# Splits of the experts' weights, each placed behind a named ACT instruction and spread over more steps

## The chip, the cores and the metric

One Trainium2 chip, and one of its cores. The metric is the device time of one execution of the kernel in microseconds (us). The engines are TensorE (PE; PEld are its weight loads), VectorE (DVE), ScalarE (ACT), GpSimd (POOL) and SyncE (SP), whose queue issues most of the DMA transfers.

## What is computed

The reference runs three layers one after the other, all in float32. Cut to what matters:

```
k_s, q_s = softmax(k over the sequence), softmax(q over the head)     # 8 batches, 8 heads, 576 x 64
x   = q_s @ (k_s^T @ v)                                               # 4608 tokens x 512
logits = x @ w_gate + log1p(exp(x @ w_noise)) * noise                 # 8 experts, the best 2 of each token
out[token] += weight * (relu(x @ w1[e]) @ w2[e])                      # w1 512 x 1024, w2 1024 x 512
h   = out @ w_in;  result = (h * cos(h)) @ w_out                      # w_in 512 x 2048, w_out 2048 x 512
```

## The kernel before

**Stages.** The span falls into these stretches. From 0 to some 125 us the keys and values are loaded and the products k^T v are formed, together with the first 18 of 36 "query columns" of 128 tokens. From 125 to some 255 us the other 18 columns follow: for each, x_t transposes 128 tokens on PE (L368), ACT takes the exponential of the transpose (tile qtt, L370), x_mm multiplies (L384, L389), and DVE divides and reduces (L392 to L398). Routing, the choice of two experts for each token, runs in three chunks beside them: the first covers columns 0 to 17, and its chain goes from ACT (L432 to L437: rs, ru, rt, rln) to DVE (L441 to L463) to ACT (rex, L469) to DVE and PE, to ACT again (W, L488) and to DVE, and it ends with a list of rows, idx (L543). With that list POOL gathers tokens for the first expert (tile xg, L618). Every token group passes an expert in "steps" of 128 of the hidden columns: mm1 (PE, L750 to L752) fills ph, ACT makes the rounded half hh of it (L756), DVE the rest hl (L757), and two steps later (LAG = 2) mm2 (L774 to L776) multiplies hh and hl by w2 into acc. At a group's end the accumulators are copied to ys, those with an even number by ACT (L785) and those with an odd number by DVE (L787). The groups of the first expert hold 2, 2, 2 and 3 blocks of 128 tokens, those of the seven others 4, 3 and 2; a tenth block is computed only when an expert has that many tokens. Each has 8 steps. The last layer runs in the same manner, as 9 groups of 4 blocks and 16 steps, with more work on ACT and DVE (kk, r) between ph and hh; its weights count as "experts" 8 and 9.

**Weights and splits.** Every weight is used as a rounded half (float32r) and a rest, w = h + l. An expert's weights come in 16 pieces of 128 x 512: SP loads a piece into one of three staging tiles wst (L141), ACT copies it to w1h or w2h, which rounds (L136), and POOL subtracts, w1l or w2l (L137). That pair is called a split here. The generator w_load has a piece loaded at each of its steps and splits the piece loaded two steps before. wbg.step(n) advances it by n: by 4 for each query column (expert 0), by 2 for each step of the first expert's last group and of the last layer, by 1 for each step of the others.

**What else runs beside the experts.** DVE turns w_in and w_out, which come as float64, into float32: 64 jobs of eight instructions (L821 to L833), whose inputs SP loads (tile c, L844) and whose results SP writes (L834, to wi_d and wo_d). They run beside the first experts only. SP also carries the DMA transposes of the gathered tokens (L645).

**Order.** Each engine works through its own queue in order. A scheduler sets that order when the program is built: it takes the instructions as the Python code issues them, simulates them, and places each where its simulation finds the engine free. `tc.issue_after(i)` bars it from placing an instruction ahead of instruction i. The transposes L677 were already placed in this way.

Of the kernel before, what the change touches and what calls it, by code (L numbers as in the profile page):

```python
# [15 lines left out]
AF = mybir.ActivationFunctionType  # L16
# [11 lines left out]
def tile_attention_moe_moe2(  # L28
# [14 lines left out]
    nc = tc.nc  # L43
# [70 lines left out]
        return res  # L114

    W = [None, None]

    def alloc_w(pool, i):
        w1h = pool.tile([P, NK, F], F32R, name=f"w1h{i}")
# [5 lines left out]
    def w_load(e):  # L125

        pend = []
        w1h, w1l, w2h, w2l = W[e % 2]

        def split():  # L130
            (kind, i, fh, _), st = pend.pop(0)
            if kind == 0:
                hi, lo = w1h[:, i, fh * 512:(fh + 1) * 512], w1l[:, i, fh * 512:(fh + 1) * 512]
            else:
                hi, lo = w2h[:, i, :], w2l[:, i, :]
            nc.scalar.activation(hi, st, AF.Copy)  # L136
            nc.gpsimd.tensor_tensor(lo, st, hi.bitcast(F32), op=ALU.subtract)  # L137

        for pc in w_pieces(e):
            st = late[0].tile([P, 512], F32, name="wst", bufs=3)  # L140
            nc.sync.dma_start(st, pc[3])  # L141
            pend.append((pc, st))
            if len(pend) == 3:
                yield
                split()
        while pend:
            yield
            split()
# [209 lines left out]
    def x_t(n):  # L358

        t, c9 = divmod(n, PC)  # L360
        pt = ps_at("pqt", "tr", 2)
        for i in range(4):
            if c9 < 8:
                b, c = 2 * t + c9 // 4, c9 % 4
                src = QE[2 * b + i // 2][:, c, 2 * (i % 2):2 * (i % 2) + 2, :]
            else:
                src = QTL[t][:, 2 * i:2 * i + 2, :]
            nc.tensor.transpose(pt[:, i * P:(i + 1) * P], src.rearrange("p h d -> p (h d)"), ident)  # L368
        qtt = at.tile([P, 4, P], F32, name="qtt", bufs=2)
        nc.scalar.activation(qtt, pt.rearrange("p (i s) -> p i s", i=4), AF.Exp)  # L370
        QTT[n] = qtt

    def x_mm(n):
# [371 lines left out]
    def mm1(g, f):  # L745
        w1h, w1l = W[(g.e if g.t is None else f // NF) % 2][:2]
        fs = slice((f % NF) * P, (f % NF + 1) * P)
        ph = ps_tr("ph", g.i < NEARLY)[:, :g.N]
        for kc in range(NK):
            nc.tensor.matmul(ph, w1h[:, kc, fs], g.xh[:, kc, :g.N], start=kc == 0, stop=False)  # L750
            nc.tensor.matmul(ph, w1h[:, kc, fs], g.xl[:, kc, :g.N], start=False, stop=False)  # L751
            nc.tensor.matmul(ph, w1l[:, kc, fs], g.xh[:, kc, :g.N], start=False, stop=kc == NK - 1)  # L752
        j = steps.index((g, f)) % (LAG + 1)
        hh, hl = HH[j][:, :g.N], HL[j][:, :g.N]
        if g.t is None:
            nc.scalar.activation(hh, ph, AF.Relu)  # L756
            after.append(nc.vector.scalar_tensor_tensor(hl, ph, 0.0, hh.bitcast(F32), op0=ALU.max, op1=ALU.subtract))  # L757
        else:
            kk = late[1].tile([P, 512], F32, name="kk", bufs=2)
            r = late[1].tile([P, 512], F32, name="r", bufs=2)  # L760
            times_cos(r, kk, ph)
            nc.scalar.activation(hh, r, AF.Copy)  # L762
            after.append(nc.vector.tensor_tensor(hl, r, hh.bitcast(F32), op=ALU.subtract))  # L763
        HT[g.i, f] = (hh, hl)

# [119 lines left out]
    def experts():  # L885

        nonlocal over
        fbg = None
        first = NEARLY * NF
        for i in range(first, len(steps) + LAG):  # L890
            if i < len(steps):
                g, f = steps[i]
                if f == 0 and g.i > NEARLY and groups[g.i - 1].more:
                    last_block(groups[g.i - 1])
                mm1(g, f)
                if f == 0 and g.e == E - 1 and g.more:

                    nc.scalar.activation(spare, HT[g.i, f][0][:, :1].bitcast(F32), AF.Sin, scale=0.0)
            if i >= first + LAG:
                mm2(*steps[i - LAG])  # L900
            if i >= len(steps):
                continue
            nxt = groups[g.i + 1] if g.i + 1 < len(groups) else None
            if g.i == NEARLY:
                if f == 2:

                    nc.gpsimd.memset(YS[0], 0.0)
                    nc.sync.dma_start(y_d[(NB - 1) * P * E:, :].rearrange("(p j) d -> p j d", p=P),
                                      YS[0][:, None, :].to_broadcast([P, E, DM]))
                if f == g.nf - 2:  # L910
                    why = "a count of experts"
                    over = nc.values_load(flag[:1, :1], min_val=0, max_val=2 * E,
                                          skip_runtime_bounds_check_because=why)
                    for e in range(E):
                        used.append(nc.values_load(flag[:1, 1 + e:2 + e], engines=USERS, min_val=0, max_val=1,
                                                   skip_runtime_bounds_check_because=why))
                if f == g.nf - 1:
                    cbg.add(convert())
            if f == (2 if g.t == 0 else 0) and nxt is not None:
                fbg = fetch(nxt)  # L920
            if fbg is not None:
                if g.t is None or f % 2 == 0:
                    next(fbg, None)
            p0 = g.nf - (2 if g.nb > 2 else 1) - (nxt.nx if nxt else 0)
            if nxt is not None and f >= p0:
                if f == p0:
                    finish(fbg)
                    pbg = prep(nxt)
                next(pbg, None)
                if f == g.nf - 1:  # L930
                    finish(pbg)
            wbg.step(2 if g.t is not None or g.e == 0 else 1)
            if g.nb > 2 or f < p0:
                cbg.step(2 if f == 0 else 1)
            if f == g.nf - 1 and nxt is not None:
                if nxt.t == 0:
                    cbg.drain()
                    wbg.drain()
                    late.pop().release()
                    late.append(tc.alloc_tile_pool(name="tp", bufs=1, reuse_waits="tile"))  # L940
                    wbg.add(w_load(E + 1))
                elif nxt.t is None and nxt.b0 == 0 and nxt.e + 1 <= E:
                    wbg.drain()
                    if nxt.e + 1 == E:
                        cbg.drain()
                    wbg.add(w_load(nxt.e + 1))
# [64 lines left out]
    for n in range(n, NCOL):  # L1011
# [10 lines left out]
                if t + 1 < NPAIR:  # L1022
                    load_tail(t + 1, "q")
        x_unit(n)
        wbg.step(4)
        if n >= 27:
            bg.step(2)
            dbg.step(1 + n % 2)
# [27 lines left out]
    left = 0  # L1056
    while dbg.q:
        dbg.step()
        left += 1
        if left >= 3:  # L1060
            next(pg, None)
# [93 lines left out]
```

## Time and profile before

| | |
|---|---|
| time, median of 3 runs | 1932.73 us (1931.42 to 1937.19) |
| the profiled execution | 1936.69 us, of which the span of the trace 1934.6 us |
| PE busy | 1815.6 us, 94% of the span |
| DVE, ACT, POOL busy | 58%, 44%, 23% of the span |
| mean granted TensorE clock | 0.962 of full speed |

Busy shares are averages over the stretches above, which have different limits. The trace names for each idle time of an engine the event that ended it: "PE acc L776 <- DVE hl L757" is PE idle ahead of the matmul of line 776 until the DVE instruction of line 757 was done. The profiled execution took 3.96 us longer than the median of the runs.

### The profile page before, as it was taken

How to read it: one execution, taken by the hardware profiler on the slowest of the kernel's cores; microseconds unless marked ns; L12 is line 12 of the kernel's file. 1: busy time of each engine (PE TensorE's matmuls, PEld its weight loads, DVE VectorE, ACT ScalarE, POOL GpSimd, SP SyncE). 2: the span in 40 equal slices, each digit the busy share in tenths (PEclk: the TensorE clock that was granted, in tenths of full speed). 3: DMA queues.
4: the chain of work that ended last, by engine and by line, in shares of the span. 5: the costliest groups of instructions: out<-in, count | busy, mean ns of one | idle time of the engine just before them, and what ended most of it. 6: DMA issues, size and time to landing. Idle time of an engine off the chain costs nothing. (4 is left out here: it accounts for less than half of the span.)

```text
span 1934.6 us, 27003 instructions
## 1 busy us (share of the span) xinstructions
PE 1815.6 (94%) x9738; PEld 1531.3 (79%) x9738; DVE 1118.6 (58%) x2138; ACT 860.6 (44%) x1514; POOL 447.7 (23%) x405
## 2 busy tenths in 40 slices
PE   5875988999899999999999999999999999999998
PEld 4764877788787788888888878888888888888886
DVE  4657677877767744334323357665656566665654
ACT  5542223313123132232424256666666666666654
POOL 6655033404114023041405143110101010110000
PEclk8775999999999999999999999999999999999999
DMA  9954246546545443252435342211212030201000
GB/s 269 291 168 129 79 128 206 186 142 192 150 125 182 141 132 115 79 155 81 133 92 148 98 139 65 71 28 60 56 33 66 23 88 16 72 28 49 1 23 23
DMA packets 179774, 206.18 MB, mean 107 GB/s; under 512 B 34224, under 2 KB 121264, under 8 KB 179632
## 3 DMA queue, kind: packets, MB, share of 16 engines
q1 hardware_dynamic: 160704, 152.17, 26.4%
q0 software_dynamic: 12160, 39.86, 7.1%
q10 hardware_dynamic: 6768, 12.32, 1.7%
q8 instruction: 82, 1.34, 0.3%
q14 instruction: 60, 0.49, 0.1%
HBM read 127.06 MB, written 49.43 MB: 91 GB/s over the span
## 5 line engine op out<-in xcount | busy, mean ns | idle before, releaser
L750 PE MATMUL ph<-xh,w1h 128*128 128x512 f32 (+2 forms) x1376 | 491.9, 357 | 6.9 <-DVE r L696 2.9
L752 PE MATMUL ph<-xh,w1l 128*128 128x512 f32 (+2 forms) x1376 | 491.3, 357 | 0.0
L751 PE MATMUL ph<-xl,w1h 128*128 128x512 f32 (+2 forms) x1376 | 490.6, 357 | 0.0
L774 PE MATMUL acc<-w2h,hh 128*128 128x512 f32 x1152 | 455.8, 396 | 17.1 <-DVE ys L787 9.7
L775 PE MATMUL acc<-w2l,hh 128*128 128x512 f32 x1152 | 453.3, 394 | 0.0
L776 PE MATMUL acc<-w2h,hl 128*128 128x512 f32 x1152 | 427.7, 396 | 21.5 <-DVE hl L757 19.7
L750 PEld LDWEIGHTS ph<-xh,w1h 128*128 128x128 f32 x1376 | 261.8, 190 | 47.1 <-DVE hl L757 4.0
L751 PEld LDWEIGHTS ph<-xl,w1h 128*128 128x128 f32 x1376 | 261.5, 190 | 38.2 <-DMA xl<-xg 0.8
L752 PEld LDWEIGHTS ph<-xh,w1l 128*128 128x128 f32 x1376 | 261.8, 190 | 32.1
L776 PEld LDWEIGHTS acc<-w2h,hl 128*128 128x128 f32 x1152 | 217.2, 190 | 73.7 <-DVE hl L757 26.1
L774 PEld LDWEIGHTS acc<-w2h,hh 128*128 128x128 f32 x1152 | 218.2, 189 | 65.7 <-ACT hh L756 11.1
L775 PEld LDWEIGHTS acc<-w2l,hh 128*128 128x128 f32 x1152 | 218.4, 190 | 40.4
L757 DVE SCALAR_TENSOR_TENSOR hl<-ph,hh 128x256 fp32r<-128x256 f32 (+2 forms) x200 | 107.1, 538 | 243.3 <-ACT hh L756 243.1
L756 ACT ACTIVATE hh<-ph 128x256 fp32r<-128x256 f32 (+2 forms) x200 | 93.9, 472 | 265.2 <-PE ph L752 250.8
L696 DVE SCALAR_TENSOR_TENSOR r<-r,ph 128x512 f32<-128x512 f32 x144 | 98.9, 687 | 151.4 <-ACT r L695 150.3
L618 POOL DMA_INDIRECT xg<-x_d,idx x80 | 76.8, 959 | 441.8 <-DVE xl L681 190.4
L694 ACT ACTIVATE r<-r 128x512 f32<-128x512 f32 x144 | 90.7, 630 | 151.9 <-DVE r L693 151.9
L763 DVE TENSOR_TENSOR hl<-r,hh 128x512 fp32r<-128x512 f32 x144 | 102.1, 709 | 86.4 <-ACT hh L762 86.3
L680 ACT ACTIVATE xh<-xg 128x512 fp32r<-128x512 f32 x106 | 66.7, 630 | 166.2 <-DVE xg L677 164.0
L137 POOL TENSOR_TENSOR w1l<-wst,w1h 128x512 fp32r<-128x512 f32 x80 | 104.9, 1326 | 137.9 <-ACT w1h L136 137.0
L618 POOL DMA_INDIRECT xg<-y_d,SL x36 | 34.3, 954 | 420.5 <-DVE xl L681 389.8
L692 DVE SCALAR_TENSOR_TENSOR r<-kk,ph 128x512 f32<-128x512 f32 x144 | 98.7, 685 | 51.6 <-ACT kk L691 50.0
(186 smaller groups left out, 2162.9 us busy)
## 6 DMA issues: line engine op xcount, KB each, us to landing
wst<-in_moe_w_dram SPq DMA_DIRECT2D x128, 256.0 KB
xl<-xg SPq DMA_DIRECT2D x396, 64.0 KB
y_d<-ys ACTq DMA_DIRECT2D x47, 256.0 KB
kt<-in_k_dram SPq DMA_DIRECT2D x16, 512.0 KB
vt<-in_v_dram SPq DMA_DIRECT2D x16, 512.0 KB
qt<-in_q_dram SPq DMA_DIRECT2D x16, 512.0 KB
x_d<-xs SPq DMA_DIRECT2D x32, 256.0 KB
c<-in_moe_w_in_dram SPq DMA_DIRECT2D x32, 256.0 KB
```

Source lines behind the costliest of these rows:

```text
L137: nc.gpsimd.tensor_tensor(lo, st, hi.bitcast(F32), op=ALU.subtract)
L618: return nc.gpsimd.indirect_dma_start(out=dst, out_offset=None, in_=src, in_offset=bass.IndirectOffsetOnAxis(ap=ix, axis=0))
L692: nc.vector.scalar_tensor_tensor(r, kk, -C1, ph, op0=ALU.mult, op1=ALU.add)
L696: nc.vector.scalar_tensor_tensor(r, r, 1.0, ph, op0=ALU.subtract, op1=ALU.mult, reverse0=True)
L750: nc.tensor.matmul(ph, w1h[:, kc, fs], g.xh[:, kc, :g.N], start=kc == 0, stop=False)
L751: nc.tensor.matmul(ph, w1h[:, kc, fs], g.xl[:, kc, :g.N], start=False, stop=False)
L752: nc.tensor.matmul(ph, w1l[:, kc, fs], g.xh[:, kc, :g.N], start=False, stop=kc == NK - 1)
L757: after.append(nc.vector.scalar_tensor_tensor(hl, ph, 0.0, hh.bitcast(F32), op0=ALU.max, op1=ALU.subtract))
L763: after.append(nc.vector.tensor_tensor(hl, r, hh.bitcast(F32), op=ALU.subtract))
L774: nc.tensor.matmul(g.acc[m], hh[:, ms], w2h[:, fr, :], start=f == 0, stop=False)
L775: nc.tensor.matmul(g.acc[m], hh[:, ms], w2l[:, fr, :], start=False, stop=False)
L776: nc.tensor.matmul(g.acc[m], hl[:, ms], w2h[:, fr, :], start=False, stop=f == g.nf - 1)
```

## The change

A list named `behind` takes every exponential of a query column (L370) and every hh (L756, and L762 in the last layer). The ACT half of each split may not be placed ahead of the last entry of that list. Three rates change: a query column advances the weights of the first expert by 2 pieces in place of 4, a step of the first expert's last group advances those of the second by 1 in place of 2, and the loop that finishes the first expert's early groups now advances them too. No instruction is added or removed but for the waits that go with the order.

```diff
     W = [None, None]
+    behind = []
...
                 hi, lo = w2h[:, i, :], w2l[:, i, :]
-            nc.scalar.activation(hi, st, AF.Copy)
+
+            with tc.issue_after(behind[-1].ins):
+                nc.scalar.activation(hi, st, AF.Copy)
             nc.gpsimd.tensor_tensor(lo, st, hi.bitcast(F32), op=ALU.subtract)
...
         qtt = at.tile([P, 4, P], F32, name="qtt", bufs=2)
-        nc.scalar.activation(qtt, pt.rearrange("p (i s) -> p i s", i=4), AF.Exp)
+        behind.append(nc.scalar.activation(qtt, pt.rearrange("p (i s) -> p i s", i=4), AF.Exp))
...
-            nc.scalar.activation(hh, ph, AF.Relu)
+            behind.append(nc.scalar.activation(hh, ph, AF.Relu))
...
-            nc.scalar.activation(hh, r, AF.Copy)
+            behind.append(nc.scalar.activation(hh, r, AF.Copy))
...
-            wbg.step(2 if g.t is not None or g.e == 0 else 1)
+            wbg.step(2 if g.t is not None else 1)
...
         x_unit(n)
-        wbg.step(4)
+        wbg.step(2)
...
     while dbg.q:
         dbg.step()
+        wbg.step()
         left += 1
```

Line numbers of the changed kernel are 3 greater than those of the kernel before from the split on.

**ACT, query columns, start of the first routing chunk.** ACT's queue in the kernel before (L136 is the copy of a split, L370 a column's exponential, L432 to L437 the start of the routing):

```order
L136 ACTIVATE w1h_1668<-wst 128x512 x3
L370 ACTIVATE qtt<-pqt 128x512
L136 ACTIVATE w1h_1668<-wst 128x512
L370 ACTIVATE qtt<-pqt 128x512
L136 ACTIVATE w2h_1670<-wst 128x512 x2
L432 ACTIVATE rs<-lg 128x144
L433 ACTIVATE ru<-rs 128x144
L435 ACTIVATE rt_1750<-ru,one 128x144
L437 ACTIVATE rln<-rt_1750 128x144
```

The same place of ACT's queue in the changed kernel:

```order
L373 ACTIVATE qtt<-pqt 128x512 x2
L139 ACTIVATE w1h_1668<-wst 128x512
L435 ACTIVATE rs<-lg 128x144
L436 ACTIVATE ru<-rs 128x144
L438 ACTIVATE rt_1742<-ru,one 128x144
L440 ACTIVATE rln<-rt_1742 128x144
```

Six splits stood ahead of rln, one does now.

**ACT, the end of the same routing chunk's part on ACT**, from rex to W, in the kernel before:

```order
L469 ACTIVATE rex<-rdl 128x18
L136 ACTIVATE w1h_1668<-wst 128x512
L136 ACTIVATE w2h_1670<-wst 128x512 x3
L370 ACTIVATE qtt<-pqt 128x512
L136 ACTIVATE w2h_1670<-wst 128x512
L488 ACTIVATE W_71<-pr 128x18
```

And in the changed kernel:

```order
L472 ACTIVATE rex<-rdl 128x18
L139 ACTIVATE w2h_1670<-wst 128x512
L373 ACTIVATE qtt<-pqt 128x512
L139 ACTIVATE w2h_1670<-wst 128x512 x2
L491 ACTIVATE W_71<-pr 128x18
```

All 16 splits of the first expert stood ahead of W, seven do now. On POOL the rests move with them: four stood ahead of the first of the last subtractions for the query softmax (tile qe, L347), one does now, and the gathers of the first group (L618) stand behind 13 rests of 16, with three more behind the gathers, where all 16 stood long before them.

**ACT, the first steps of the second expert's first group** (4 blocks), in the kernel before (L785 is the copy of the group before, L790 its write, hh the rounded half of a step):

```order
L136 ACTIVATE w1h_1668<-wst 128x512 x3
L785 ACTIVATE ys_1683<-acc 128x512
L790 DMA y_d<-ys_1683 128x512
L136 ACTIVATE w1h_1668<-wst 128x512
L756 ACTIVATE hh_1677<-ph 128x512
L756 ACTIVATE hh_1675<-ph 128x512
L136 ACTIVATE w2h_1670<-wst 128x512
L785 ACTIVATE ys_1681<-acc 128x512
L136 ACTIVATE w2h_1670<-wst 128x512 x2
L790 DMA y_d<-ys_1681 128x512
L756 ACTIVATE hh_1676<-ph 128x512
```

And in the changed kernel:

```order
L139 ACTIVATE w2h_3114<-wst 128x512
L788 ACTIVATE ys_1683<-acc 128x512
L793 DMA y_d<-ys_1683 128x512
L139 ACTIVATE w2h_3114<-wst 128x512 x2
L759 ACTIVATE hh_1677<-ph 128x512
L759 ACTIVATE hh_1675<-ph 128x512
L139 ACTIVATE w1h_1668<-wst 128x512
L788 ACTIVATE ys_1681<-acc 128x512
L793 DMA y_d<-ys_1681 128x512
L759 ACTIVATE hh_1676<-ph 128x512
L139 ACTIVATE w1h_1668<-wst 128x512
L759 ACTIVATE hh_1677<-ph 128x512
```

The last four splits of the second expert's own weights (w2h_3114) now stand here, and from the second step on one split of the third expert's (w1h_1668) follows each hh; the 16 splits last for the 16 steps of the groups of 4 and 3 blocks, where they stood in the first 8 steps or so. The same holds for the experts after it. In the first steps of the last layer no split stands ahead of the first kk any more, where five did.

**DVE, the end of the second expert's group of 4 blocks**, in the kernel before (L757 is hl, L787 the copy of an accumulator, L821 and L822 begin a conversion job whose input SP loads):

```order
L757 SCALAR_TENSOR_TENSOR hl_1679<-ph,hh_1676 128x384
L757 SCALAR_TENSOR_TENSOR hl_1680<-ph,hh_1677 128x384
L821 TENSOR_SCALAR ca<-c_5321 128x256
L787 COPY ys_1683<-acc 128x512
L822 TENSOR_SCALAR ca<-ca 128x256
```

And in the changed kernel:

```order
L760 SCALAR_TENSOR_TENSOR hl_1679<-ph,hh_1676 128x384
L760 SCALAR_TENSOR_TENSOR hl_1680<-ph,hh_1677 128x384
L790 COPY ys_1683<-acc 128x512
L824 TENSOR_SCALAR ca<-c_5321 128x256
L825 TENSOR_SCALAR ca<-ca 128x256
```

The copy stood behind the first instruction of a conversion; it stands ahead of it now, and so at the same place of the third and the fourth expert. SP's loads of weights, which stood in bursts, are spread over the steps, and some stand among the DMA transposes of the groups. The order of PE's own instructions hardly changes.

## Rows read from the trace of the kernel before

**Rows 1.** The page's part 1: busy us, share of the span, instructions.

```profile
PE 1815.6 (94%) x9738; PEld 1531.3 (79%) x9738; DVE 1118.6 (58%) x2138; ACT 860.6 (44%) x1514; POOL 447.7 (23%) x405
```

**Rows 2.** Windows: stretch, us; PE, PEld, DVE, ACT, POOL busy; clock, DMA, GB/s.

```profile
125.00:199.00 74.00, 45.03 (x434) 37.95 (x431) 53.59 (x150) 21.88 (x45) 35.98 (x29) 0.63 0.45 137
199.00:255.00 56.00, 55.91 (x465) 47.87 (x464) 37.77 (x141) 13.97 (x34) 3.48 (x6) 1.00 0.19 63
255.00:335.00 80.00, 67.77 (x373) 58.76 (x372) 61.30 (x124) 23.81 (x46) 33.17 (x29) 0.96 0.59 192
335.00:700.00 365.00, 336.87 (x1655) 286.23 (x1655) 268.00 (x602) 95.53 (x191) 91.34 (x78) 0.97 0.52 159
700.00:1140.00 440.00, 439.70 (x2271) 383.45 (x2270) 151.50 (x238) 140.14 (x274) 125.21 (x108) 1.00 0.37 111
1140.00:1170.00 30.00, 24.81 (x99) 19.04 (x98) 22.65 (x23) 23.12 (x41) 23.33 (x20) 0.94 0.74 212
1170.00:1935.00 765.00, 756.07 (x3332) 624.93 (x3330) 449.91 (x668) 474.42 (x775) 59.22 (x57) 1.00 0.14 42
```

**Rows 3.** Waits, 125 to 199 us: waiter, releaser; us in total, times, longest.

```profile
PE pqt L368 <- ACT qtt L370: 18.2, 8, 4.9
...
ACT w1h L136 <- DMA wst<-in_moe_w_dram: 9.6, 4, 4.8
ACT w2h L136 <- DMA wst<-in_moe_w_dram: 8.6, 4, 3.7
```

**Rows 4.** Timeline of ACT, 139 to 165 us: start, us, instruction, [idle before, releaser].

```profile
139.97 0.63 ACT L136 ACTIVATE w1h<-wst 128x512 fp32r<-128x512 f32 x1 [4.80 <-DMA wst<-in_moe_w_dram]
...
162.50 1.31 ACT L136 ACTIVATE w2h<-wst 128x512 fp32r<-128x512 f32 x2 [3.73 <-DMA wst<-in_moe_w_dram]
...
164.71 0.18 ACT L488 ACTIVATE W<-pr 128x18 f32<-128x18 f32 x1
```

**Rows 5.** Timeline of DVE and POOL, 141 to 186 us.

```profile
143.84 1.22 DVE L344 TENSOR_REDUCE qm<-qt 128x16 f32<-128x1024 f32 x1 [5.36 <-POOL qe L347]
...
164.92 0.46 DVE L426 TENSOR_TENSOR rw<-rm,pr 128x288 f32<-128x288 f32 x1 [4.51 <-ACT W L488]
...
185.76 1.14 POOL L618 DMA_INDIRECT xg<-x_d,idx  x1 [12.63 <-DVE idx L543]
```

**Rows 6.** Waits of PE and ACT, 255 to 335 us.

```profile
ACT w2h L136 <- DMA wst<-in_moe_w_dram: 14.6, 5, 6.7
...
PE acc L776 <- DVE hl L757: 5.2, 2, 3.5
...
PE acc L774 <- ACT hh L756: 3.1, 3, 1.7
```

**Rows 7.** Waits of ACT and PE, 335 to 700 us.

```profile
ACT w2h L136 <- DMA wst<-in_moe_w_dram: 34.5, 17, 4.5
...
PE acc L776 <- DVE hl L757: 14.6, 11, 2.2
...
PE acc L774 <- DVE ys L787: 9.7, 3, 3.7
```

**Rows 8.** Timeline of DVE and PE at a group's end, 515 to 517 us.

```profile
515.32 0.29 DVE L821 TENSOR_SCALAR ca<-c 128x256 int32<-128x256 int32 x1 [5.38 <-DMA c<-in_moe_w_out_dram]
...
516.27 0.78 PE L774 MATMUL acc<-w2h,hh 128*128 128x512 f32 x1 [3.42 <-DVE ys L787]
```

**Rows 9.** Timeline of DVE and POOL, 365 to 369 us.

```profile
365.05 4.44 DVE L831 TENSOR_SCALAR ca<-cb 128x256 int32<-128x256 int32 x1
...
365.53 1.31 POOL L137 TENSOR_TENSOR w1l<-wst,w1h 128x512 fp32r<-128x512 f32 x1
366.78 2.55 POOL L137 TENSOR_TENSOR w2l<-wst,w2h 128x512 fp32r<-128x512 f32 x2
```

**Rows 10.** All instructions of DVE line 831: least, median, greatest ns.

```profile
L831 DVE TENSOR_SCALAR ca<-cb x64: 252/289/4440, 267.1 to 694.0; 128x256 int32<-128x256 int32 x64
```

**Rows 11.** Wait of PE, 1140 to 1170 us.

```profile
PE ph L750 <- DVE r L696: 2.9, 2, 2.7
```

## Prediction, made before the changed kernel ran

> **What bounds the kernel now.** I read the busy shares first, then the stretches, then the waits of each stretch that has gaps. PE is busy for 1815.6 us, 94% of the span [rows 1], and the change leaves PE's instructions as they are. So time can come only from two places: PE's idle time, and matmuls that run below full clock after a gap. The stretches show where these lie [rows 2]. From 125 to 199 us PE is busy for 45.0 of 74 us, at a mean clock of 0.63. From 199 to 255 us it is full. From 255 to 335 us it idles for 80 - 67.8 = 12.2 us, from 335 to 700 us for 28.1 us, from 1140 to 1170 us for 5.2 us. From 700 to 1140 us it is busy for 439.7 of 440 us at clock 1.00, and after 1170 us for 756.1 of 765 us. So the splits of the later experts, which the change moves just as much, have nothing to win: whatever waits there is hidden behind a full PE. Clocks of 0.96, 0.97 and 0.94 in the three stretches with gaps cost a further 0.04 x 80 = 3.2 us, 0.03 x 365 = 11 us and 0.06 x 30 = 1.8 us against 1.00 (2.4 GHz; a mean below it holds parts at the lower level, 1.2 GHz).
>
> **The change part by part.** Splits are neither removed nor added: the same ACT copies and POOL rests run, in other places. What counts is who stands behind them in a queue, because a split can begin only when its piece of weights has landed.
>
> A, query columns (125 to 199 us). ACT stands still for 9.6 + 8.6 = 18.2 us ahead of splits whose piece has not landed, up to 4.8 us at a time, and PE stands still for 18.2 us ahead of transposes that need a buffer freed by qtt [rows 3]. The routing's instructions on ACT queue behind those splits too. ACT waited 4.80 us for the piece of the split at 139.97 us and 3.73 us for that at 162.50 us, and W came right behind the second, at 164.71 us [rows 4]. The routing on DVE was held twice: its next work, ahead of the routing, waited 5.36 us for POOL's qe, which had four rests ahead of it; and later DVE waited 4.51 us for W [rows 5]. The gathers, which start the first expert, waited on POOL for the end of that chain, 12.63 us, and went at 185.76 us [rows 5]. From then on PE fills. So these 5.36 + 4.51 = 9.9 us lie on the path. In the new order one split instead of six stands ahead of rln, seven instead of sixteen ahead of W, and one rest instead of four ahead of qe. I take -8 us, since a few splits, and what waits for loads, remain. Most that can come is the 9.9 us and one more wait of 4.8 us for a piece, ahead of a qtt: -14 us. The other end: the gathers now stand behind 13 rests on POOL. If the routing gains nothing and one such 4.8 us wait falls ahead of them, that is +5 us. POOL's 12.63 us of waiting ahead of the gathers covers the later rests otherwise; if the routing is 8 us earlier, 4 us of that cover are left, about one wait for a piece.
>
> B, first expert (255 to 335 us). ACT waits 14.6 us in five times for pieces of w2h that stand ahead of an hh, and PE then waits 3.1 us for hh and 5.2 us for hl, which needs hh [rows 6]. In the new order each split comes behind an hh, and its piece has a step to land. I take all of the 3.1 us, half of the 5.2 us (the rest goes with conversions on DVE) and 1.3 of the 3.2 us of clock: -7 us. Ends: 0, and all idle time with the clock, 12.2 + 3.2 = 15.4 us.
>
> C, second to fourth expert (335 to 700 us), where the conversions run. Three waits with 9.7 us together are for the copies of accumulators on DVE, and 14.6 us in eleven times are for hl [rows 7]. The first sort is plain: a copy stands behind the first instruction of a conversion, which waited 5.38 us for its input, and PE idled 3.42 us and went on with a matmul of 0.78 us [rows 8]. In the new order the copy is ahead, so I take -8 of the 9.7 us. Of the hl waits I take -4: ACT's waits for pieces, 34.5 us in 17 times [rows 7], go from ahead of hh to behind it, but conversions and POOL's rests still hold DVE. With fewer gaps about a third of the 11 us of clock comes back: -4 us. Against that, 8 of 16 splits of each expert now fall into its 3-block group, where all stood in the 4-block group before; I add +4 us, by this: one conversion instruction took 4.44 us at 365.05 us, until just after POOL's rests ended at 366.78 + 2.55 = 369.33 us [rows 9], where the median of its line is 0.289 us [rows 10]. It was held by three rests, so by (4.44 - 0.29) / 3 = 1.4 us for one rest at worst. Eight rests in three experts then cost DVE up to 33 us; DVE has 365 - 268 = 97 us idle there [rows 2], so I let one in eight through to PE. C: -8 - 4 - 4 + 4 = -12 us. Ends: everything gained, 28.1 + 11 = -39 us; and +33 us.
>
> The Trainium skill has a rule for this, on the page "SBUF — State Buffer", section "Who interferes with whom": GpSimd and the second port of VectorE are one shared pair, held as an exclusive lock, so that the later of two such instructions is blocked for the whole of the other. Row and rule agree that DVE stands still, but by the rule one rest should block one instruction, while here one instruction was held through several. By the rule taken strictly the number of locks stays at 16 an expert and the change gains nothing on them; the sum would then be 4 us less favourable on the hl waits.
>
> D, start of the last layer (1140 to 1170 us). PE waits 2.9 us for r [rows 11] because five splits, waiting for their pieces, stood ahead of the first kk on ACT; none does now. I take -4 us with some of the clock; ends 0 and 5.2 + 1.8 = -7 us.
>
> The waits that go with the order cost nothing of their own: a split waits for an instruction ahead of it in the same queue. Queued behind a split on ACT are the next hh or qtt, and SP's later loads, since SP waits with a load for a free staging tile, with the c loads and the DMA transposes behind it. That is part of the rivals' price.
>
> Sum: -8 - 7 - 12 - 4 = -31 us. Against the profiled execution (1936.7 us) that is 1905.7 us; the median of the runs stands 4.0 us lower, so 1932.7 - 31 = 1902 us.
>
> **The rivals.**
> R1, the stalls of the second to fourth expert remain. What holds hl is DVE, not ACT: conversions and rests of POOL, of which as many run as before. A copy that no longer waits behind a conversion then waits for DVE to come through its queue. For it: PE's waits there are on DVE for 9.7 + 14.6 us [rows 7]. Against it: the 5.38 us in rows 8 are a wait for a load, with DVE empty. C is 0, A, B and D stand: -19 us, 1914 us.
>
> R2, no change. The pieces land as late as before, since loads are issued no earlier relative to their split; a late piece then holds the next hh in place of this one, and the routing's end is held by something else, such as its PE and DVE work. For it: the waits for pieces in all stretches are long [rows 3, 6, 7]. Against it: the splits now have about twice the time to come, and DMA is at 0.45 to 0.59 of its share in these stretches [rows 2]. Within 6 us of 1932.7: I put it at 1930 us.
>
> R3, slower: the rests hold DVE in the 3-block groups. There a step is shorter than in a 4-block group, and conversions, transposes of the next group and hl fill more of it. If each of the 24 rests costs DVE the 1.4 us of rows 9, and DVE is then behind by more than the two steps that mm2 leaves it, PE waits for all of it: C is +33 us in place of -12, and with A, B and D the sum is +14 us: 1947 us. It decides from the point at which DVE's idle time in such a group falls to nothing; over the whole stretch DVE has 27% idle [rows 2], which speaks against it. The same page of the Trainium skill speaks for it, since an exclusive lock is paid once for each rest wherever it stands.
>
> **How the numbers follow.** The forecast, 1902 us with its own range of 1884 to 1910 us, has 0.52. More than that, under 1884 us (C near its end), 0.05. R1 0.20, R2 0.11, R3 0.12. Faster by over 0.3% (5.8 us, about what a measurement of this kernel can tell from no change) is the first three, 0.77; same is R2, 0.11; slower is R3, 0.12. The range runs from 1884 us, which leaves out 0.05, to 1932 us, which takes in R1 and R2 and leaves out R3: 0.17 in all.
>
> **What the profile of the changed kernel would show.** A: DVE's waits for qe and W are under 2 us together, and the first gather stands near 177 us, without a wait for a rest ahead of it. B: between the stretch's counterparts PE waits under 1 us for hh. C: the three waits for ys are gone, PE's waits for hl are under 11 us, and DVE's conversions in the 3-block groups have some single instructions of over 1 us. D: the first kk is on ACT before any split and PE's wait for r is under 1 us. PE is full from 700 us on as before, so what A to D gain reaches the end whole. The prediction is wrong if the gathers wait for rests, if hl waits grow in the 3-block groups, or if hh still waits for late pieces ahead of it.

## The result, and the profile after

The changed kernel takes 1944.84 us in the median of 6 runs (1942.15 to 1947.84), the kernel before, run beside it, 1933.66 us (1931.42 to 1937.19). The ratio is 1.0056, with a 95% interval of 1.0042 to 1.0071: slower by some 11 us, where 31 us less were forecast. The profiled execution is one of the fastest of the changed kernel, 1942.27 us with a span of 1940.2 us, 5.6 us above the span before. The account by stretches below is of these 5.6 us; the rest of the 11 us lies in the other executions, which were not traced.

PE's busy time and share, from the page after (PE, PEld, DVE, ACT, POOL; compare [rows 1]):

```profile
PE 1821.3 (94%) x9738; PEld 1535.4 (79%) x9738; DVE 1130.0 (58%) x2138; ACT 853.7 (44%) x1514; POOL 451.6 (23%) x405
```

The same stretches as in [rows 2], of the changed kernel (stretch, its length, busy us of PE, PEld, DVE, ACT and POOL with the number of instructions, mean granted clock, DMA share, GB/s):

```profile
125.00:199.00 74.00, 52.32 (x466) 43.53 (x465) 59.93 (x160) 22.70 (x48) 36.83 (x29) 0.58 0.45 140
...
255.00:335.00 80.00, 71.14 (x390) 62.23 (x388) 57.40 (x134) 23.65 (x47) 32.92 (x28) 0.98 0.63 200
335.00:700.00 365.00, 324.63 (x1563) 274.71 (x1562) 279.92 (x577) 88.76 (x181) 91.56 (x79) 0.95 0.51 155
700.00:1140.00 440.00, 439.85 (x2290) 384.92 (x2290) 151.50 (x246) 137.25 (x279) 122.30 (x105) 1.00 0.37 111
1140.00:1170.00 30.00, 27.37 (x112) 21.66 (x111) 17.74 (x23) 20.91 (x36) 17.38 (x15) 0.94 0.64 176
```

From 335 to 700 us PE is busy for 324.6 us, where it was 336.9 us, at a clock of 0.95 in place of 0.97, and DVE for 279.9 us in place of 268.0. From 255 to 335 us it went the other way (71.1 us for 67.8), and from 700 us on PE is as full as before. The waits of that long stretch in the changed kernel (waiter, releaser; us in total, times, longest), beside [rows 7]:

```profile
PE acc L779 <- DVE hl L760: 35.3, 16, 4.8
...
ACT w2h L139 <- DMA wst<-in_moe_w_dram: 3.2, 2, 1.7
...
PE acc L777 <- DVE ys L790: 1.3, 2, 0.9
```

ACT's waits for pieces of w2h went from 34.5 to 3.2 us and PE's waits for the copies ys from 9.7 to 1.3 us, both as the change has it. But PE's waits for hl went from 14.6 to 35.3 us, up to 4.8 us at a time.

Since the work moves in time, windows at fixed times mix stages. The next table takes the start of each hl in DVE's timeline as a mark (344 of them, in the same order in both kernels; read to 0.1 us) and gives the time between marks, in us:

| from ... to ... | before | after | change | forecast |
|---|---|---|---|---|
| start to the first hl (query columns, first routing chunk) | 200.9 | 198.4 | -2.5 | -8 (A) |
| first expert | 144.1 | 138.9 | -5.2 | -7 (B) |
| second to fourth expert | 367.4 | 382.7 | +15.3 | -12 (C) |
| of it: the three groups of 4 blocks | 147.5 | 146.2 | -1.3 | |
| of it: the three groups of 3 blocks | 110.6 | 137.3 | +26.7 | |
| of it: the three groups of 2 blocks | 109.2 | 99.2 | -10.0 | |
| fifth to seventh expert | 324.3 | 325.3 | +1.0 | 0 |
| eighth expert and the first half of the last layer's first group | 152.6 | 150.9 | -1.7 | -4 (D) |
| the rest of the last layer, to its last hl | 734.5 | 733.3 | -1.2 | 0 |

The loss is in the groups of 3 blocks, 8 to 9.5 us in each of the three that run beside conversions. The fifth to seventh expert have the same new order of splits and take 0.3 us more each.

One such place in the changed kernel, in the third expert's group of 3 blocks: rows of the timeline of DVE, POOL and PE (start, us, instruction; in brackets the idle time before it and what ended it):

```profile
539.31 4.48 DVE L828 SCALAR_TENSOR_TENSOR cb<-c,cb 128x256 int32<-128x256 int32 x1
...
544.12 0.55 DVE L760 SCALAR_TENSOR_TENSOR hl<-ph,hh 128x384 fp32r<-128x384 f32 x1
...
538.82 0.96 POOL L621 DMA_INDIRECT xg<-x_d,idx  x1 [3.54 <-DVE cb L826]
539.80 3.70 POOL L140 TENSOR_TENSOR w2l<-wst,w2h 128x512 fp32r<-128x512 f32 x3
...
544.72 0.79 PE L779 MATMUL acc<-w2h,hl 128*128 128x512 f32 x1 [4.77 <-DVE hl L760]
```

POOL's gather came at 538.82 us, and the three rests queued behind it ran without a break from 539.80 to 543.50 us. DVE's conversion instruction of line 828 began at 539.31 us, while the gather still ran, and was held until 543.79 us. The hl behind it started at 544.12 us, and PE, which needed it, had idled for 4.77 us. That is the hold of [rows 9], but in a group where no rest ran before. The rests and DVE's busy time in that group, between marks, first the rests alone (stretch, length, POOL busy with the count, clock, DMA, GB/s), before and after:

```profile
509.00:545.00 36.00, 0.00 (x0) 0.95 0.48 142
```

```profile
507.00:553.00 46.00, 8.85 (x7) 0.93 0.50 152
```

and then all engines (as in [rows 2]), before and after:

```profile
509.00:545.00 36.00, 32.58 (x162) 29.06 (x162) 26.86 (x72) 5.49 (x11) 2.84 (x3) 0.95 0.48 142
```

```profile
507.00:553.00 46.00, 35.85 (x164) 29.75 (x164) 36.38 (x73) 9.94 (x20) 11.73 (x10) 0.93 0.50 152
```

No rest ran in it before, seven are recorded now, and DVE is busy for 36.4 us where it was busy for 26.9. That is (36.4 - 26.9) / 7 = 1.4 us for one rest, the price that the prediction had worked out from one block, and the group is 9.5 us longer. DVE's idle time in these windows is no free time either: all of its waits there are for the input of a conversion (tile c), and what stands behind that conversion in DVE's queue, hl too, waits with it. DVE's waits in the window of before, then in that of after:

```profile
DVE ca L821 <- DMA c<-in_moe_w_out_dram: 8.2, 6, 5.4
```

```profile
DVE ca L824 <- DMA c<-in_moe_w_out_dram: 8.8, 4, 5.1
```

So DVE was working or waiting for a conversion's input for 26.9 + 8.2 = 35.1 of 36 us before, and for 36.4 + 8.8 = 45.2 of 46 us after.

### The profile page after: what moved, and what is told of

The parts are those of the page before. It is cut to its first block, busy times and chain, and to the rows that moved or that the text cites. A ratio compares the mean times of both kernels' runs of the same rounds, so it can differ in the third digit from the quotient of the medians.

```text
span 1940.2 us, 27004 instructions
## 1 busy us (share of the span) xinstructions
PE 1821.3 (94%) x9738; PEld 1535.4 (79%) x9738; DVE 1130.0 (58%) x2138; ACT 853.7 (44%) x1514; POOL 451.6 (23%) x405
## 5 line engine op out<-in xcount | busy, mean ns | idle before, releaser
L753 PEld LDWEIGHTS ph<-xh,w1h 128*128 128x128 f32 x1376 | 262.3, 191 | 45.8 <-DVE hl L760 5.0
```

## The experiments

Three theories stood at the start. Theory 1: POOL's rests hold DVE's conversions, and with them the hl that PE needs. Theory 2: the new rates did it, not the order. Theory 3: the conversions and transposes ahead of hl take up DVE by themselves. "The second to fourth expert" is always the time between the same marks as in the table: 367.4 us before, 382.7 us after.

**The order without the rates, and the rates without the order.**

```diff
-            wbg.step(2 if g.t is not None else 1)
+            wbg.step(2 if g.t is not None or g.e == 0 else 1)
...
         x_unit(n)
-        wbg.step(2)
+        wbg.step(4)
...
         dbg.step()
-        wbg.step()
```

> The change with its issue_after, but with the three old rates (4 pieces a query column, 2 a step of the first expert's last group, none in the loop of the early groups). Theory 1 (POOL's rests, which the new order queues in threes behind a waiting gather, hold DVE's conversions and so hl): the order in the second to fourth expert is that of the changed kernel, so PE waits there for hl for 30 to 40 us, and only what lies before 335 us differs; 1944 to 1950 us. Theory 2 (the rates do it): the time goes back to within 4 us of 1933.7 us.

Measured: 1950.03 us, 1.0070 of before (1.0047 to 1.0094). The second to fourth expert take 384.5 us, and PE's waits for hl from 335 to 700 us are

```profile
PE acc L779 <- DVE hl L760: 34.7, 18, 4.8
```

The other half:

```diff
-            with tc.issue_after(behind[-1].ins):
-                nc.scalar.activation(hi, st, AF.Copy)
+            nc.scalar.activation(hi, st, AF.Copy)
```

> The three new rates without the issue_after. The scheduler places splits where its simulation finds ACT free, so the order of ACT and POOL hardly differs from before. Theory 1: within 4 us of before, 1930 to 1937 us, PE's waits for hl in the second to fourth expert 12 to 18 us. Theory 2 (the rates do it): 1940 to 1946 us.

Measured: 1938.40 us, 1.0015 of before (1.0001 to 1.0029), and the second to fourth expert take 367.7 us. Its waits there:

```profile
PE acc L778 <- DVE hl L759: 13.5, 11, 2.3
...
PE acc L776 <- DVE ys L789: 11.9, 3, 4.5
```

The time lies between the two forecasts, 1.4 us above that of theory 1, but the kernel before took 1935.50 us beside it, and the waits are those of theory 1. So the order does it and the rates do next to nothing alone; theory 2 falls. The order with the old rates and with the new ones can't be told apart: the intervals of their ratios overlap.

**The order given up where the conversions run.**

```diff
-            with tc.issue_after(behind[-1].ins):
+            if e in (2, 3, 4):
                 nc.scalar.activation(hi, st, AF.Copy)
+            else:
+                with tc.issue_after(behind[-1].ins):
+                    nc.scalar.activation(hi, st, AF.Copy)
```

> The changed kernel, but the splits of the third, fourth and fifth expert, which run beside the second to fourth expert and beside nearly all conversions, have no issue_after. Theory 1: the loss of some 17 us between 335 and 700 us goes and the gains elsewhere (2.6 us in the query columns, 5 in the first expert, 3.5 at the start of the last layer) stay: 1920 to 1927 us, PE's waits for hl there 12 to 18 us. If those gains came only from a shift that is given back later, 1930 to 1936 us.

Measured: 1930.14 us, 0.9969 of before (0.9956 to 0.9982). The second to fourth expert take 371.4 us, with waits of the kind from before:

```profile
PE acc L782 <- DVE hl L763: 17.1, 12, 3.8
...
PE acc L780 <- DVE ys L793: 11.6, 3, 4.5
```

The loss is gone with the order there, as theory 1 has it. The time is 3 us above that range and lies in that of the other case, in which the gains elsewhere were only a shift: they are smaller than the trace of the changed kernel let me think. In this trace the first hl comes at 200.2 us, only 0.7 us earlier than before, and the first expert takes 3.5 us less.

**Short rests, in both kernels.** Theory 1 against theory 3.

```diff
-            nc.gpsimd.tensor_tensor(lo, st, hi.bitcast(F32), op=ALU.subtract)
+            nc.gpsimd.tensor_tensor(lo[:, :64], st[:, :64], hi.bitcast(F32)[:, :64], op=ALU.subtract)
...
-            nc.tensor.matmul(ph, w1l[:, kc, fs], g.xh[:, kc, :g.N], start=False, stop=kc == NK - 1)
+            nc.tensor.matmul(ph, w1h[:, kc, fs], g.xh[:, kc, :g.N], start=False, stop=kc == NK - 1)
```

(and w2h for w2l in the same manner)

> The changed kernel with the rests on POOL cut to 64 of their 512 columns; the products take the rounded halves in place of the rests, so that what is left out is not read (the result leaves out the rests). The same instructions otherwise. Theory 1: without long rests on POOL no conversion is held for over 1 us, PE's waits for hl in the second to fourth expert fall from 35 us to under 10 us, 1912 to 1922 us. Theory 3 (conversions and transposes ahead of hl fill DVE by themselves, whatever POOL does): those waits stay over 25 us, 1938 to 1945 us.

Measured: 1905.95 us, 0.9837 of before (0.9807 to 0.9867). The second to fourth expert take 354.5 us, 28.2 us less than with whole rests; the stretch from 335 to 700 us and PE's waits for hl in it:

```profile
335.00:700.00 365.00, 343.62 (x1733) 291.70 (x1732) 239.43 (x596) 97.33 (x204) 47.11 (x80) 1.00 0.52 160
```

```profile
PE acc L779 <- DVE hl L760: 15.3, 17, 2.0
```

> The kernel before with the same cut of the rests to 64 columns (the result leaves out the rests). Theory 1: rests hold DVE in the kernel before too, only less often ahead of an hl; PE's waits for hl in the second to fourth expert fall from 14.6 us to under 8 us, the waits for ys (9.7 us, for a load) stay, 1922 to 1928 us. Theory 3: no change, 1930 to 1936 us.

Measured: 1913.97 us, 0.9885 of before (0.9866 to 0.9904). The second to fourth expert take 353.0 us, 14.4 us less than before:

```profile
PE acc L774 <- DVE ys L787: 12.4, 3, 5.8
...
PE acc L776 <- DVE hl L757: 4.3, 5, 2.8
```

Both say the same. With short rests the two orders differ by 354.5 - 353.0 = 1.5 us in the second to fourth expert, with whole rests by 15.3 us. So of the loss 13.8 us are the rests: they cost 14.4 us there in the old order and 28.2 us in the new one. All instructions of line 828, which was held in the rows above, after and with short rests (count; least, median and greatest ns):

```profile
L828 DVE SCALAR_TENSOR_TENSOR cb<-c,cb x64: 371/424/4478, 263.6 to 683.4; 128x256 int32<-128x256 int32 x64
```

```profile
L828 DVE SCALAR_TENSOR_TENSOR cb<-c,cb x64: 370/424/550, 262.9 to 683.1; 128x256 int32<-128x256 int32 x64
```

With the same count and median the longest went from 4478 to 550 ns. Theory 3 in its pure form falls: both times are even below the ranges of theory 1, by 6 and 8 us. But something is left of it: with short rests too these experts take 354 us, where 325 us are possible (below), and PE still waits 15.3 us for hl in the changed order, more than the 10 us that theory 1 expected.

**Gathers behind the rests**, so that rests no longer pile up behind a gather that waits for DVE:

```diff
-            nc.gpsimd.tensor_tensor(lo, st, hi.bitcast(F32), op=ALU.subtract)
+            rests.append((nc.gpsimd.tensor_tensor(lo, st, hi.bitcast(F32), op=ALU.subtract), tc.nc.cur_bb))
...
-        return nc.gpsimd.indirect_dma_start(out=dst, out_offset=None, in_=src,
-                                            in_offset=bass.IndirectOffsetOnAxis(ap=ix, axis=0))
+        late_ok = rests and rests[-1][1] is nc.cur_bb
+        with tc.issue_after(rests[-1][0].ins) if late_ok else nullcontext():
+            return nc.gpsimd.indirect_dma_start(out=dst, out_offset=None, in_=src,
+                                                in_offset=bass.IndirectOffsetOnAxis(ap=ix, axis=0))
```

> The changed kernel, with each gather barred from standing ahead of the last rest that the code has issued by then, so that fewer rests queue behind a gather that waits for DVE. Theory 1 with the weight on the row of three rests behind one gather: PE's waits for hl in the second to fourth expert fall from 35 us to under 22 us, 1926 to 1938 us. If single rests cost as much in sum as three in a row, 1941 to 1948 us. Theory 3: no change, 1941 to 1948 us.

Measured: 1950.03 us, 1.0074 of before (1.0049 to 1.0099). The total is above every expected range. In the second to fourth expert the time fell (371.6 us, 11.1 us less than after), and the waits for hl halved as expected, while those for ys came back:

```profile
PE acc L781 <- DVE hl L762: 18.7, 10, 3.6
...
PE acc L779 <- DVE ys L792: 16.6, 3, 7.2
```

But the first hl came at 206.0 us, 7.6 us later than after, and the first expert took 147.2 us, 8.3 us more, because the edit also put the first expert's early gathers behind 16 rests. So the total said nothing on the question, and I ran it again without that:

```diff
+        x_d_late[0] = g.i > NEARLY and g.t is None
...
-        late_ok = rests and rests[-1][1] is nc.cur_bb
+        late_ok = x_d_late[0] and rests and rests[-1][1] is nc.cur_bb
```

> The changed kernel, with the gathers of the experts' later groups alone barred from standing ahead of the last rest; the first expert's early gathers are left where the change has them. If the loss of the earlier try with all gathers came from the early ones (first hl 7.6 us and the first expert's end a further 8.4 us later), those stretches are as in the changed kernel, the second to fourth expert as in that try (some 372 us in place of 383), and the time is 1932 to 1938 us. If it came from gathers that come too late for the next group, 1943 us or more.

Measured: 1935.18 us, 1.0012 of before (0.9995 to 1.0029). The first hl is at 197.6 us, the first expert takes 143.2 us, still 4.3 us more than after, and the second to fourth expert take 373.4 us, 9.3 us less. Not all of the 9 to 11 us by which these experts became faster in the two runs need be the rests in threes: the conversions moved too, and in both runs under 2 jobs are left in the fourth expert's group of 3 blocks, where 7 ran after. In the other two such groups, with 7 jobs and 7 rests as after, the time in the last run is 41.5 and 40.9 us, in place of 46.3 and 45.8 us. That is some 5 us of the 9 us that each of them had lost.

**Fewer conversions in a step, behind hl.** If DVE is the limit, its other work is what should be moved; after[-1] is the last hl. The last job gets the same edge.

```diff
                 yield
-                z = half1()
+                with tc.issue_after(after[-1].ins):
+                    z = half1()
                 yield
-                half2(*z)
+                with tc.issue_after(after[-1].ins):
+                    half2(*z)
...
```

Before, the scheduler had drawn the conversions forward, to 262 us in the changed kernel, and done them beside the first to fourth expert. With this edge they come where the code issues them: half a job of eight instructions a step, beside the second to seventh expert.

> The changed kernel, and each half of a conversion barred from standing ahead of the last hl on DVE; by this order conversions run half a job a step beside the second to seventh expert, behind hl, in place of beside the first to fourth. Theory 1: a conversion that is held then no longer holds the hl of its own step, and there are half as many in a step, so the gaps between 335 and 700 us mostly go without new ones between 700 and 1100 us: 1895 to 1910 us. Theory 3: the same, 1895 to 1910 us. Rival: late conversions hold hl as much, only later: 1930 us or more.

Measured: 1875.64 us, 0.9687 of before (0.9669 to 0.9706). Three stretches, as in [rows 2]:

```profile
255.00:335.00 80.00, 76.97 (x424) 67.43 (x423) 27.16 (x58) 26.16 (x52) 33.74 (x30) 0.98 0.52 163
335.00:700.00 365.00, 364.72 (x1869) 317.69 (x1868) 249.60 (x498) 109.62 (x219) 104.91 (x90) 1.00 0.50 152
700.00:1140.00 440.00, 437.22 (x2241) 380.05 (x2240) 256.23 (x463) 163.07 (x313) 142.29 (x120) 1.00 0.46 138
```

PE is busy for 364.7 of 365 us at full clock, with the splits in the order of the change and eight rests in each group of 3 blocks. The second to fourth expert take 324.8 us, 58 us less than after, and the first expert, beside which no conversion runs now, 130.8 us in place of 138.9. The gain is larger than expected, since I had counted idle time and clock of the kernel before by windows and not the first expert's share. Rests still hold conversions, but DVE has time for it, and none of DVE's waits from 335 to 700 us is for a conversion's input any more. The longest instruction of line 828 is now about one rest long:

```profile
L828 DVE SCALAR_TENSOR_TENSOR cb<-c,cb x64: 416/425/1400, 334.0 to 948.4; 128x256 int32<-128x256 int32 x64
```

> The kernel before with the same order of the conversions. The gaps between 335 and 700 us (28 us and the clock) mostly go, those of the query columns, the first expert and the start of the last layer stay: 1902 to 1915 us, and 5 to 12 us more than the changed kernel with that order, which is what the change's order of the splits is worth where DVE is not the limit. If the splits ahead of hh cost nothing there, the two are within 4 us.

Measured: 1885.32 us, 0.9744 of before (0.9724 to 0.9763). So the change's order of the splits is worth about 10 us once DVE has room: 1875.64 against 1885.32 us, both on one chip, in intervals of the ratio that do not touch. In the traces 1.6 us of it lie ahead of the first hl, 1.8 us in the first expert and 1.6 us around the start of the last layer; the rest is in no single place of the traces, whose spans differ by 3.4 us only (the one traced is the longest of the four executions in the first kernel and the shortest in the second).

**The place behind hl, or the number in a step?** That edit changed both.

```diff
-                cbg.step(2 if f == 0 else 1)
+                cbg.step(4 if f == 0 else 2)
```

> The changed kernel with the conversions behind hl, and advanced twice as fast, so that a whole job of eight instructions comes in a step and most of them run beside the second to fourth expert, as in the changed kernel. If it is the place behind hl that cures the stall, the second to fourth expert take under 335 us (325 with half a job a step, 383 in the changed kernel) and the time is under 1890 us. If it is the smaller number of conversions in a step, they take 350 us or more and the time is over 1905 us.

Measured: 1940.55 us, 1.0027 of before (1.0013 to 1.0041). The second to fourth expert take 388.0 us, the groups of 3 blocks alone 141.4 us:

```profile
335.00:700.00 365.00, 323.02 (x1556) 273.86 (x1555) 304.00 (x656) 85.81 (x176) 88.96 (x77) 0.94 0.53 162
700.00:1140.00 440.00, 439.70 (x2286) 384.08 (x2286) 150.51 (x244) 137.37 (x278) 121.61 (x104) 1.00 0.37 110
```

```profile
PE acc L779 <- DVE hl L760: 21.0, 14, 4.5
...
PE acc L777 <- DVE ys L790: 17.1, 3, 7.1
```

With the same edge behind hl but a whole job a step all of it is back. So the place behind hl alone does not cure the stall; the smaller number of conversions in a step does, with that place. The smaller number without it was not run. In the groups of 3 blocks, where PE needs 34.1 us, DVE is busy for 27 us with 4 to 5 jobs and 8 rests, for 27 us with 7 jobs and no rest (before), for 35 to 36 us with 7 jobs and 7 recorded rests (after), and for 40 to 41 us with 8 to 9 jobs and 7 or 8 rests.

What a conversion costs there is not its work alone. DVE's waits for inputs of conversions from 335 to 700 us, before and after:

```profile
DVE ca L821 <- DMA c<-in_moe_w_out_dram: 33.9, 23, 5.4
DVE ca L821 <- DMA c<-in_moe_w_in_dram: 23.9, 14, 5.6
```

```profile
DVE ca L824 <- DMA c<-in_moe_w_in_dram: 29.3, 13, 7.3
DVE ca L824 <- DMA c<-in_moe_w_out_dram: 26.1, 15, 5.6
```

That is 57.8 us before and 55.4 us after, some 33 us with a whole job a step behind hl, and nothing with half a job. How much of the gain is fewer conversions ahead of hl, and how much is inputs that have landed by then, no run here separates.

**A slower start of the first expert's weights**, with the conversions behind hl, beside that kernel once more.

```diff
-        wbg.step(2)
+        wbg.step(1 if n < 27 else 2)
```

> The changed kernel with the conversions behind hl, and the first expert's weights advanced by 1 piece for each of the first nine of these query columns and by 2 after them; six rests in place of thirteen stand ahead of the first gather. If rests beside the routing's work on DVE give back part of what the earlier routing gains (its DVE part from rw to idx takes 24.6 us in the changed kernel, 20.4 us before), the first hl comes 2 to 4 us earlier: 1871 to 1874 us. If the later rests hold the first expert's steps instead, 1876 to 1880 us.

> The changed kernel with the conversions behind hl once more, beside the run with the slower first expert: 1873 to 1880 us.

Measured: 1877.63 us (0.9705, 0.9683 to 0.9726) and 1876.46 us (0.9697, 0.9675 to 0.9719): no difference. The first hl came 2.8 us earlier, at 197.7 us, as the first expectation has it, but the next 16 steps took 67.0 us in place of 65.3, as the second has it. The kernel with the conversions behind hl, at 1876 us twice, is the best version that I found; it beats both kernels by 3% or more.

## Why the prediction was wrong

**The step that failed is the +4 us in C**, "I let one in eight through to PE". The price of a rest was right: 1.4 us by one block of [rows 9], 1.4 us by the group after. So was the place: of the eight rests in each group of 3 blocks seven are recorded between the marks, and R3's 24 x 1.4 = 33 us has its counterpart in the +26.7 us of these groups. Wrong was what became of it. I took DVE's idle time over the whole stretch, 97 of 365 us, as the cover. But the rests land in three groups only. In the one shown above 36 - 26.9 = 9.1 us were idle before, and eight rests at 1.4 us are 11.2 us: the idle time falls to nothing there, the point from which by the prediction R3 decides, and I had not worked it out for that window. Nor was the idle time a cover: 8.2 of the 9.1 us, and 57.8 of the 97 us, were DVE waiting for the input of a conversion. So nearly all of the rests' time went through to PE in these groups, and not one in eight. The 2-block groups gave 10 us back. Three rests left each of them (not all 16 stood in the 4-block group before, as the prediction has it), and conversions ran earlier. So R3 is the case that held, with its mechanism and place, and less than its price: C came to +15.3 us, not +33. That its 1947 us is so near to the measured 1944.84 us is in part luck: C lost 18 us less, and A, B and D gained some 10 us less, than its sum has them.

**What was right in C.** The copies: -8 us forecast, 9.7 to 1.3 us measured. The hl waits behind late pieces went too, as ACT's 34.5 to 3.2 us shows, but other hl waits took their place, as R1 has it in kind. "Waits for hl under 11 us" was the mark for right or wrong, and 35.3 us is the answer.

**A, -8 forecast, -2.5 measured.** The routing was freed as worked out: W came behind seven splits in place of sixteen, and DVE's rw came at 157.08 us, 7.8 us earlier than in [rows 5]. Then 4.2 us went back, since from rw to idx DVE took 24.6 us, where it was 164.92 to 185.30 = 20.4 us before. The row of idx before:

```profile
185.30 0.17 DVE L543 CAST idx<-rit 128x4 int32<-128x4 f32 x1
```

Rows of DVE and POOL from that part, after:

```profile
157.08 0.46 DVE L429 TENSOR_TENSOR rw<-rm,pr 128x288 f32<-128x288 f32 x1 [0.31 <-ACT W L491]
...
161.88 3.48 DVE L429 TENSOR_TENSOR bl<-eq,tx 128x480 bf16<-128x480 bf16 x2
...
165.40 1.99 DVE L429 TENSOR_TENSOR eq<-ioe,RBL 128x480 bf16<-128x480 bf16 x1
...
181.64 0.96 DVE L546 CAST idx<-rit 128x4 int32<-128x4 f32 x1
...
161.51 2.21 POOL L350 TENSOR_TENSOR qe<-qt,qm 128x1024 f32<-128x1024 f32 x1
163.68 1.42 POOL L140 TENSOR_TENSOR w1l<-wst,w1h 128x512 fp32r<-128x512 f32 x1
165.06 2.06 POOL L350 TENSOR_TENSOR qe<-qt,qm 128x1024 f32<-128x1024 f32 x1
...
181.30 1.27 POOL L140 TENSOR_TENSOR w2l<-wst,w2h 128x512 fp32r<-128x512 f32 x1
182.88 1.14 POOL L621 DMA_INDIRECT xg<-x_d,idx  x1 [0.32 <-DVE idx L546]
```

The two steps of line 429 (bl, then eq) and the cast are long where POOL's qe and rests run: eq takes 1.99 us here, where such an eq took 0.40 us elsewhere in the same trace. The first gather came at 182.88 us, 2.9 us earlier. The step that failed is that the sum ended at W: the part from W to idx was taken as fixed, while the change moved POOL's work into it. The run with fewer rests there moved the first hl by another 2.8 us and lost that in the steps after; it does not change the total. (The far end of A, -14 us, is -14.7 us by its own terms.)

**B, -7 forecast, -5.2 measured**, and the kind is right. The waits after, from 255 to 335 us, beside [rows 6]:

```profile
ACT w2h L139 <- DMA wst<-in_moe_w_dram: 9.8, 6, 2.3
...
PE ph L753 <- DVE hl L760: 3.8, 1, 3.8
...
PE acc L779 <- DVE hl L760: 2.5, 1, 2.5
...
PE acc L777 <- ACT hh L759: 0.5, 1, 0.5
```

PE's waits for hh fell from 3.1 to 0.5 us. What stands is hl. The runs with the conversions behind hl show what holds it: with hardly a conversion beside it the first expert of the changed kernel takes 128 to 132 us, in place of 138.9 us.

**D, -4 forecast, -1.7 measured.** No split stands ahead of the first kk, but PE's wait for r, which I took for their effect [rows 11], hardly changed:

```profile
PE ph L753 <- DVE r L699: 2.5, 1, 2.5
```

The wait was not for the splits alone; what else sets it no run here told.

**The clock.** A third of 11 us was to come back as gaps closed. Gaps opened, and the mean went from 0.97 to 0.95. With half a job of conversions in a step, where PE has no gaps, it is 1.00 over the same 365 us. Of the 43 us between 367.4 and 324.8 us some 15 us are that by estimate: the other 28 us are PE's idle time in [rows 2].

**The Trainium skill's rule** (page "SBUF — State Buffer", section "Who interferes with whom": one port pair that VectorE and GpSimd share, an exclusive lock for a whole instruction) spoke for R3 in the prediction. The trace agrees that DVE stands still beside POOL's rests. Read strictly, as one rest that blocks one instruction, it does not fit: one instruction of DVE was held through three rests in a row, 4.48 us.

**Share of the causes.** Shown by runs: that the order and not the rates costs the time, that the rests' length is 13.8 of the 15.3 us, and that half the conversions in a step, behind hl, remove all of it. Shown in part: that piles behind a gather are some 5 us in each of two groups. Argued only: that the 2-block groups became faster because their rests left. Open: how the gain of fewer conversions divides between DVE's work and its waits for inputs, the 5 us by which the medians differ more than the two traces, and what sets the wait at the start of the last layer.

## What to carry to other kernels

Before work is spread over more steps, look at the stage that receives it: take the busy time of the engine that it holds in that window, not in the average over the stretch, and put the engine's own time per step beside PE's. Ask what the engine's idle time there is: idle time in which it stands at the head of its queue for an input covers nothing (8.2 of 9.1 us here). Where a wait ends on DVE, count POOL's element-wise work as DVE work beside it; in the group above one rest of 1.2 to 1.3 us cost DVE 1.4 us. And when an engine has nothing left in one stage and much in the next, moving its background work (here conversions, from 7 jobs to 4 or 5 in a group) can be worth far more than reordering what stands in front of it: here 3% against 0.5%.

## What the runs showed of the hardware that I had not expected

An instruction of DVE that meets POOL's element-wise work can be held through several POOL instructions in a row: 4.48 us through three rests (3.70 us together) and the last half microsecond of the gather ahead of them, with a median of 0.42 us for its line. With the conversions behind hl in the changed kernel, the longest hold of a conversion was 1.4 us. The rows fit a loop that feeds itself, which is argued and not shown: a DVE that is late frees a buffer late, POOL's gather waits for that buffer, rests queue up behind the gather, and they then run in one block that holds DVE for longer. In the runs with the later gathers behind the rests, two groups of 3 blocks with the same jobs and rests became some 5 us shorter each.
